# Second batch: masks written by TensorE and one exponential a pair; seven weight conversions in which ScalarE makes the three low bits

## The chip, the cores and the metric

The kernel runs on one core of one Trainium2 chip. The metric is the device time of one execution in microseconds (us), shown as the median of the runs. The kernel before takes 871.65 us, the median of three runs (871.54, 871.65 and 874.05).

## The reference

Eight batches, eight heads, 576 tokens, head size 64. Attention looks at 32 keys: the last 32 tokens in the first four heads, every fourth of the last 128 in the others. Its output, 4608 tokens of 512, goes through a feed-forward block with an ELU between two products. Everything is float32.

```python
scores = scale * q @ k.T                      # scale = 1/8, masked outside the window
attn = exp(scores - max(scores)); attn /= attn.sum(-1) + 1e-9
x = (attn @ v) as 4608 x 512
h = x @ w_in                                  # 512 x 2048
out = where(h > 0, h, exp(min(h, 0)) - 1) @ w_out    # 2048 x 512
```

The weights are drawn as float64, and are read from HBM as 64-bit integers. The kernel makes float32 of them itself.

## The kernel before, in words

Tokens go in chunks. The first chunks (`CS` = 3) have 512 tokens each; the later ones are done in another form that this change does not touch. A chunk's first product goes over 16 slices `f` of the inner 2048: `product1` makes h(f) in a PSUM bank (`h0` or `h1` in turn while c = 0), `elu` makes the ELU of it (ScalarE: Exp and then Relu; VectorE: the combination with h, at L632 or L634), and `second_product`, some slices later, adds that slice's four 128-token tiles to the four `o_ps` banks. The chunk c = 0, some 31 to 133 us into the span, has three more jobs beside these products:

- **Conversion of the weights.** `load_w` brings two slices of 64-bit words into a block `r` of a ring; a piece `j` (0 to 7) is four rows of such words. `magnitude` (L129, ScalarE, L136) reads the upper word of each as float32 and scales its exponent, into `a`. `convert` (L138) then runs three passes on VectorE: a shift left by 3 (L144), the sign from the upper word (L152), the three low bits from the lower word (L154). Piece 0 is done in parts of 512, 512 and 1024 columns, piece 1 in two parts of 1024, each later piece in one of 2048.
- **Splits.** From slice `F1` = 3 on, the weights and x are taken as a sum of two parts (cast on ScalarE L191, difference on VectorE L193; of x, `xall`, L589 and L590).
- **Attention of the second batch** (`second_attention`): four pairs of heads. Step E does the scores of a pair into the two `a_ps` banks and the beginning of its softmax (`exponentials`), X its end (`probabilities`), O the products with v. E0 stands behind slice 1, E1 behind 3, O0 behind 5, E2 behind 7, O1 behind 9, E3 behind 11, O2 and O3 behind 14 and 15. In `exponentials`, `masks_added` (L397, VectorE) adds the mask while it brings the scores from PSUM to the tile `sm`, of which there is one; L410 takes the maximum of 12 groups of 64 columns, L413 scales it, and L389 runs an exponential for each of the 12 groups on ScalarE, which also sums it. Then GpSimd normalises, VectorE transposes, and ScalarE and GpSimd copy to `pt`, which the products read.

The first batch's attention writes its masks by a matmul of an identity with the mask ahead of the scores (bf16, 96x384), which then add to it.

TensorE's order is the one in which the program is written (`mm` keeps it). The order on VectorE and ScalarE comes from a scheduler, apart from what is kept in place with `inorder` or held behind an instruction with `issue_after`. `masked` and `maxima` are two such instructions: the second part of a conversion is held behind the newest in `maxima`, the split of x for c = 0 behind `masked`.

Of the kernel before, what the change touches and what calls it, by code (L numbers as in the profile page):

```python
# [70 lines left out]
DOWN = 2.0 ** -112  # L71
# [3 lines left out]
def body(ctx: ExitStack, tc: tile.TileContext, q, k, v, masks, w_in, w_out, out):  # L75
    nc = tc.nc
# [12 lines left out]
    mask_sb = masks_sb[:, :2 * NU * 2 * G].rearrange("p (d m) -> p d m", d=2)  # L89
    ones_sb = masks_sb[:, 2 * NU * 2 * G:]  # L90
# [9 lines left out]
    raw2, raw, full4, full2, full = [None] * (NF // 2), [None] * NF, [None] * (NF // 2), [None] * NF, [None] * 2 * NF  # L100
# [9 lines left out]
    def mm(*args, **kw):  # L110
        return inorder(nc.tensor.matmul(*args, **kw))  # L111
# [12 lines left out]
    def words(j):  # L124

        u = raw2[j].rearrange("p t c -> p (t c)").bitcast(U32).rearrange("p (c two) -> p c two", two=2)
        return u[:, :, 0], u[:, :, 1]

    def magnitude(k):  # L129
        j, part = k // 2, slice(k % 2 * 2 * DM, (k % 2 + 1) * 2 * DM)  # L130
        if k % 2 == 0:
            full4[j] = wst.tile([P, 4, DM], F32, name=f"a{j}")
        full2[k] = full4[j][:, k % 2 * 2:k % 2 * 2 + 2, :]
        for t in range(2):
            full[need[2 * k + t]] = full2[k][:, t, :]
        return nc.scalar.activation(out=full4[j].rearrange("p t c -> p (t c)")[:, part], in_=words(j)[1][:, part].bitcast(F32), func=AF.Copy, scale=DOWN)  # L136

    def convert(j, keep=lambda ins: ins, part=slice(0, 4 * DM), behind=None):  # L138

        lo, hi = [u[:, part] for u in words(j)]  # L140
        a = full4[j].rearrange("p t c -> p (t c)")[:, part]
        au = a.bitcast(U32)

        keep(nc.vector.tensor_scalar(out=au, in0=au, scalar1=3, scalar2=None, op0=ALU.logical_shift_left))  # L144
        if behind is not None:

            with tc.issue_after(behind):
                return upper_and_lower(lo, hi, au, keep)
        return upper_and_lower(lo, hi, au, keep)

    def upper_and_lower(lo, hi, au, keep):
        keep(nc.vector.scalar_tensor_tensor(out=au, in0=hi, scalar=0x80000000, in1=au, op0=ALU.bitwise_and, op1=ALU.bitwise_or))  # L152

        return keep(nc.vector.scalar_tensor_tensor(out=au, in0=lo, scalar=29, in1=au, op0=ALU.logical_shift_right, op1=ALU.bitwise_or))  # L154
# [110 lines left out]
    qk_of, v_of = {}, {}  # L265
# [28 lines left out]
    def scores(s_ps, qt, kt, start):  # L294

        for n in range(NU):
            for c in range(GU):
                for h in range(2):
                    score(s_ps[h][:, n * 2 * G:(n + 1) * 2 * G], qt, kt, h, n, c, start, start or n == NU - 1)
# [38 lines left out]
    def first_attention(hp, loaded):  # L338
# [18 lines left out]
        if hp > 0:  # L357
            load_w(hp, mx)
        inorder(nc.vector.tensor_tensor(out=sm.rearrange("p (h n) j -> p h n j", h=2), in0=s4,
                                        in1=mx4.unsqueeze(3).broadcast_to([QB, 2, NU, 2 * G]), op=ALU.subtract))  # L360
        inorder(nc.scalar.activation(out=sm, in_=sm, func=AF.Exp, scale=0.125))
        yield
# [22 lines left out]
        a_ps = ps_f.tile([P, 2, TC], F32, name="db"[hp % 2])  # L385
        yield outputs(0, hp, [(a_ps[:, i, :], i * NA, (i + 1) * NA) for i in range(NU // NA)], vt, tr, inorder)

    def exponential(u, sm, nmx, sums):
        nc.scalar.activation(out=sm[:, u, :], in_=sm[:, u, :], func=AF.Exp, bias=nmx[:, u:u + 1], scale=0.125, accum_out=sums[:, u:u + 1])  # L389

    def masks_added(hp, places, sm, eng=nc.vector):

        dil = hp >= NPAIR // 2
        for i in range(max(len(p) for p in places)):
            for h in range(2):
                n0, n1, s_ps = places[h][i]
                last = eng.tensor_tensor(out=sm[:, h * NU + n0:h * NU + n1, :].rearrange("p n j -> p (n j)"), in0=s_ps[:QB, :(n1 - n0) * 2 * G],  # L397
                                        in1=mask_sb[:, int(dil), n0 * 2 * G:n1 * 2 * G], op=ALU.add)
        return last

    def exponentials(b, hp, places, sm=None):

        if sm is None:
            sm = ap.tile([QB, 2 * NU, 2 * G], F32, name="sm", bufs=1)
            last = masks_added(hp, places, sm)
            if b == 1:
                masked.append(last.ins)
        nmx = ap.tile([QB, 2 * NU], F32, name="nmx", bufs=4)
        sums = ap.tile([QB, 2 * NU], F32, name="sums", bufs=4)
        nc.vector.tensor_reduce(out=nmx, in_=sm, op=ALU.max, axis=mybir.AxisListType.X)  # L410
        if b == 1:

            maxima.append(nc.vector.tensor_scalar(out=nmx, in0=nmx, scalar1=-0.125, scalar2=None, op0=ALU.mult).ins)  # L413
            for u in range(NU):
                exponential(u, sm, nmx, sums)
        else:
            nc.vector.tensor_tensor(out=sm, in0=sm, in1=nmx.unsqueeze(2).broadcast_to([QB, 2 * NU, 2 * G]), op=ALU.subtract)
            nc.scalar.activation(out=sm, in_=sm, func=AF.Exp, scale=0.125)
            nc.vector.tensor_reduce(out=sums, in_=sm, op=ALU.add, axis=mybir.AxisListType.X)
        return b, hp, sm, nmx, sums  # L420

    def probabilities(b, hp, sm, nmx, sums):

        if b == 1:

            for u in range(NU, 2 * NU):
                exponential(u, sm, nmx, sums)
        normalise(nc.gpsimd if b == 1 else nc.vector, sm, sums, lambda ins: ins)
        tr = transposed()
        for r in range(2):  # L430
            part = sm[:, :, r * G:(r + 1) * G]
            nc.vector.transpose(out=part, in_=part)  # L432
            for c in range(GU):
                ks, cs, rs = slice((c + r) * G, (c + r + 1) * G), slice(c * G, (c + 1) * G), slice(r * G, (r + 1) * G)
                last_transpose[b] = (nc.gpsimd.tensor_copy if r else nc.scalar.copy)(out=tr[ks, :, cs], in_=sm[cs, :, rs]).ins  # L435
        return b, hp, tr
# [55 lines left out]
    def later_probabilities(b, hps, groups):  # L492
# [9 lines left out]
        def steps(j):  # L502
# [73 lines left out]
    masked, maxima = [], []  # L576
# [43 lines left out]
    def elu(h_ps, c, f, v=nc.vector, a=nc.scalar):  # L620
        e = fp.tile([P, TC], F32, name="e")
        if 0 < c < B - 1:
# [58 lines left out]
    o_of, done = {}, {}  # L681
# [222 lines left out]
    def second_attention():  # L904

        x32[1] = xp.tile([P, NPAIR, S], F32, name="x32", bufs=2)
        state = [None] * NPAIR

        for step in " E0 X0 E1 X1 O0  E2 X2 O1  E3 X3  O2 O3".split(" "):
            if step:  # L910
                what, hp = step[0], int(step[1])
                i = NPAIR + hp
                if what == "E":
                    s_ps = banks()
                    scores(s_ps, *qk_of.pop(i), True)
                    state[hp] = exponentials(1, hp, [[(0, NU, a)] for a in s_ps])
                    load_qk(i + 1)
                    if hp == 0:
                        load_v(i + 1)
                    if hp == NPAIR - 1:  # L920
                        load_qk(i + 2)
                elif what == "X":
                    state[hp] = probabilities(*state[hp])
                else:
                    b, _, tr = state[hp]
                    places = [(a, i * NA, (i + 1) * NA) for i, a in enumerate(banks())]
                    products(places, v_of.pop(NPAIR + hp), tr)
# [9 lines left out]
    for what in "m0 qk0 qk1 qk2 qk3 v0 v1 w0 v2 v3".split():  # L937
        i = int(what[-1])
# [12 lines left out]
    for what in "S0 S1 M0 M1 S2 P0 M2 T0 U0 S3 P1 P2 A0 M3 T1 U1 O0 T2 U2 P3 B0 O1 T3 U3 O2 G0 G1 O3 G2 A1 C0 D1".split():  # L951
        i = int(what[1])
# [17 lines left out]
    load_v(NPAIR)  # L970
    for j in range(2 * (NR - NE), 2 * NR + 2):
        load_w(j)
# [12 lines left out]
    for c in range(CS):  # L985
# [14 lines left out]
        for f in range(NF):  # L1000
            while c == 0 and ready < min(NF, f + AHEAD):
                for j in (ready, ready + 1):
# [56 lines left out]
            if f in when:  # L1059
                i = when.index(f)  # L1060
# [78 lines left out]
```

## Time and profile before

| | |
|---|---|
| median of 3 runs | 871.65 us |
| the profiled execution | 872.5 us |
| its span in the trace | 870.7 us |
| mean granted clock | 0.996 |
| TensorE busy | 853.7 us, 98% |
| VectorE busy | 555.7 us, 64% |
| ScalarE busy | 526.9 us, 61% |
| GpSimd busy | 75.0 us, 9% |

The profiled execution is 1.8 us longer than its span, and 0.85 us longer than the median. The rows of the trace give a start in us from the span's beginning, a length, and behind an arrow what ended an engine's idle time. Where work on an engine follows without a wait, one row's start lies a little ahead of the end of the row before it.

### The profile page before, as it was taken

Reading aid. Unit: us, or ns where it says so; the run is one execution under the profiler, and the core shown is the slowest. Engines: PE = TensorE matmul, PEld = TensorE weight load, DVE = VectorE, ACT = ScalarE, POOL = GpSimd, SP = SyncE. Lnnn points to the kernel's source line nnn. Section 1 sums busy time; section 2 is a strip of 40 time slices with the busy share of each in tenths; the row PEclk is TensorE's granted clock in tenths of the full one; section 3 lists DMA queues with packets and bytes.
Section 4 is the critical chain, followed back from the end, with each engine's and each line's share of the span. In section 5 each row is a group of like instructions: output and inputs, shape, how many; then the busy total and the mean of one; then the engine's idle time right before and its main releaser. Section 6 shows DMA issues by size and latency. Waiting matters only on the chain.

```text
span 870.7 us, 17559 instructions
## 1 busy us (share of the span) xinstructions
PE 853.7 (98%) x6788; PEld 722.5 (83%) x6788; DVE 555.7 (64%) x902; ACT 526.9 (61%) x1031; POOL 75.0 (9%) x112
## 2 busy tenths in 40 slices
PE   6999999999999999999999999999999999999998
PEld 4556878888878889888878898988899988999986
DVE  6899987766685857787765577545476635344431
ACT  3767987756585756667654575654566654555541
POOL 2013311000020200111010020100011100000000
PEclk8999999999999999999999999999999999999999
DMA  9997335134546346867753867662875652776441
GB/s 343 378 381 264 132 123 188 34 132 133 176 160 200 102 151 215 262 221 239 231 173 100 279 200 242 212 184 83 265 226 175 206 164 80 241 209 191 143 153 56
DMA packets 93459, 166.48 MB, mean 191 GB/s; under 512 B 9696, under 2 KB 40768, under 8 KB 93376
## 3 DMA queue, kind: packets, MB, share of 16 engines
q1 hardware_dynamic: 89200, 158.01, 57.0%
q10 hardware_dynamic: 4176, 7.34, 2.3%
q8 instruction: 54, 0.88, 0.4%
q14 instruction: 29, 0.24, 0.1%
HBM read 124.42 MB, written 40.89 MB: 190 GB/s over the span
## 4 chain that ended last, share of the span: by engine, by line
PE 84%; DVE 7%; ACT 4%; DMA 2%; issue 2%; POOL 1%; SPq 0%; ACTq 0%; DVEq 0%; POOLq 0%
PE o_ps L111 41%; PE h L111 34%; PE a_ps L111 8%; DVE a L152 1%; DMA out<-e 1%; POOL pt L435 1%; DVE a L154 1%; DMA r<-combined 1%; DVE nmx L410 1%; ACT sm L389 0%; ACT pt L383 0%; DVE sm L397 0%; PE a L111 0%; DMA kt<-k 0%; DVE a L144 0%
## 5 line engine op out<-in xcount | busy, mean ns | idle before, releaser
L111 PE MATMUL h<-xall,r 128*128 128x384 f32 (+1 forms) x708 | 156.9, 363 | 0.4 <-DVE e L634 0.2
L111 PEld LDWEIGHTS h<-xall,r 128*128 128x128 f32 x708 | 127.7, 188 | 17.2 <-issue 0.8
L111 PE MATMUL o_ps<-a,gh 128*128 128x512 f32 x394 | 129.0, 416 | 0.0
L448 DVE SCALAR_TENSOR_TENSOR a-1_3369<-a-1_3369,a 128x768 f32<-128x768 f32 x64 | 61.0, 953 | 87.9 <-ACT a L448 87.9
L111 PE MATMUL h<-r,r 128*128 128x384 f32 x476 | 108.3, 337 | 0.4 <-DMA r<-combined 0.4
L448 ACT COPY e<-h 128x384 f32<-128x384 f32 x96 | 46.0, 479 | 98.5 <-PE h L111 96.6
L111 PEld LDWEIGHTS o_ps<-a,gh 128*128 128x128 f32 x394 | 73.4, 188 | 21.8 <-issue 9.1
L448 ACT ACTIVATE a<-a-1_3369 128x384 f32<-128x384 f32 (+1 forms) x96 | 60.8, 634 | 50.0 <-DVE a-1_3369 L448 44.0
L111 PEld LDWEIGHTS h<-r,r 128*128 128x128 f32 x476 | 84.4, 188 | 4.0 <-ACT e L448 0.7
L111 PE MATMUL o_ps<-r,gh 128*128 128x512 f32 x242 | 75.4, 393 | 0.0
L111 PE MATMUL o_ps<-a,r 128*128 128x512 f32 x288 | 72.3, 392 | 0.0
L111 PE MATMUL o_ps<-a,gl 128*128 128x512 f32 x173 | 67.7, 391 | 0.0
L448 ACT ACTIVATE a<-a 128x768 f32<-128x768 f32 (+1 forms) x72 | 60.8, 845 | 1.9
L111 PEld LDWEIGHTS o_ps<-a,r 128*128 128x128 f32 x288 | 53.7, 188 | 9.9
L111 PE MATMUL h<-a,r 128*128 128x384 f32 x256 | 60.1, 336 | 0.0
L448 DVE TENSOR_TENSOR a-1_3369<-h,e 128x384 f32<-128x384 f32 x64 | 35.2, 550 | 34.8 <-PE h L111 34.7
L111 PEld LDWEIGHTS o_ps<-r,gh 128*128 128x128 f32 x242 | 44.9, 188 | 8.6
L111 PEld LDWEIGHTS h<-a,r 128*128 128x128 f32 x256 | 46.4, 188 | 4.2
L111 PE MATMUL o_ps<-r,gl 128*128 128x512 f32 x117 | 46.0, 393 | 0.2 <-DVE gl L448 0.2
L435 POOL COPY pt<-sm 32x384 f32<-32x384 f32 x36 | 32.9, 913 | 103.1 <-DVE sm L432 102.1
L111 PE MATMUL o_ps<-a,xall 128*128 128x512 f32 x153 | 39.5, 393 | 0.0
L637 DVE SCALAR_TENSOR_TENSOR e<-h,e 128x512 f32<-128x512 f32 x30 | 20.9, 696 | 27.1 <-ACT e L636 27.1
(219 smaller groups left out, 1553.6 us busy)
## 6 DMA issues: line engine op xcount, KB each, us to landing
r<-combined SPq DMA_DIRECT2D x224, 256.0 KB, 3.6
aside<-a-1_3369 SPq DMA_DIRECT2D x64, 192.0 KB, 3.4
vt<-v SPq DMA_DIRECT2D x30, 384.0 KB, 4.4
kt<-k SPq DMA_DIRECT2D x30, 304.0 KB, 4.9
qt<-q SPq DMA_DIRECT2D x30, 288.0 KB, 4.2
r<-w_in SPq DMA_DIRECT2D x16, 512.0 KB, 7.9
r<-w_out SPq DMA_DIRECT2D x16, 512.0 KB, 8.3
combined<-a SPq DMA_DIRECT2D x20, 256.0 KB, 3.2
```

The costliest lines, as they stand in the source:

```text
L111: return inorder(nc.tensor.matmul(*args, **kw))
L152: keep(nc.vector.scalar_tensor_tensor(out=au, in0=hi, scalar=0x80000000, in1=au, op0=ALU.bitwise_and, op1=ALU.bitwise_or))
L154: return keep(nc.vector.scalar_tensor_tensor(out=au, in0=lo, scalar=29, in1=au, op0=ALU.logical_shift_right, op1=ALU.bitwise_or))
L410: nc.vector.tensor_reduce(out=nmx, in_=sm, op=ALU.max, axis=mybir.AxisListType.X)
L435: last_transpose[b] = (nc.gpsimd.tensor_copy if r else nc.scalar.copy)(out=tr[ks, :, cs], in_=sm[cs, :, rs]).ins
L448: return lambda *args, **kw: inorder(getattr(self.eng, name)(*args, **kw))
L637: v.scalar_tensor_tensor(out=e, in0=h_ps, scalar=0.0, in1=e, op0=ALU.max, op1=ALU.subtract)
```

## The change

Masks: in step E of the second batch TensorE writes the mask into each bank first, and the scores add to it. VectorE takes the maximum of each bank straight from PSUM (6 groups), and subtracts it on the way to `sm`. ScalarE runs one exponential of 768 columns a pair, VectorE sums its groups. Conversions: for the pieces 1 to 7 `magnitude` issues one more pass on ScalarE, `low_bits`: it reads the upper 16 bits of each lower word as an integer, scales them so that rounding leaves the top three bits, and writes these over the low 16 bits of the upper word, in place. VectorE then needs one pass for the sign and the low bits together, in place of two.

```diff
+LOW = (1, 2, 3, 4, 5, 6, 7)
...
+    def low_bits(j, part):
+        h = raw2[j].rearrange("p t c -> p (t c)").bitcast(U16).rearrange("p (c four) -> p c four", four=4)[:, part]
+        return nc.scalar.activation(out=h[:, :, 2], in_=h[:, :, 1], func=AF.Copy, scale=2.0 ** -13, bias=2.0 ** -14 - 0.5)
...
-        return nc.scalar.activation(out=full4[j]..., in_=words(j)[1][:, part].bitcast(F32), func=AF.Copy, scale=DOWN)
+        done = nc.scalar.activation(out=full4[j]..., in_=words(j)[1][:, part].bitcast(F32), func=AF.Copy, scale=DOWN)
+        return low_bits(j, part) if j in LOW else done
...
+    def upper_and_lower(j, lo, hi, au, keep):
+        if j in LOW:
+            return keep(nc.vector.scalar_tensor_tensor(out=au, in0=hi, scalar=0x80000007, in1=au, op0=ALU.bitwise_and, op1=ALU.bitwise_or))
         keep(nc.vector.scalar_tensor_tensor(out=au, in0=hi, scalar=0x80000000, in1=au, op0=ALU.bitwise_and, op1=ALU.bitwise_or))
         return keep(nc.vector.scalar_tensor_tensor(out=au, in0=lo, scalar=29, in1=au, op0=ALU.logical_shift_right, op1=ALU.bitwise_or))
...
     def exponentials(b, hp, places, sm=None):
         if b == 1:
-            maxima.append(nc.vector.tensor_scalar(out=nmx, in0=nmx, scalar1=-0.125, scalar2=None, op0=ALU.mult).ins)
-            for u in range(NU):
-                exponential(u, sm, nmx, sums)
+            heads = [(slice(h * NU, (h + 1) * NU), a[:QB, :NU * 2 * G].rearrange("p (n j) -> p n j", n=NU)) for h, a in enumerate(places)]
+            for part, s3 in heads:
+                nc.vector.tensor_reduce(out=nmx[:, part], in_=s3, op=ALU.max, axis=mybir.AxisListType.X)
+                last = nc.vector.tensor_tensor(out=sm[:, part, :], in0=s3, in1=wide(nmx[:, part], NU), op=ALU.subtract)
+            masked.append(last.ins)
+            maxima.append(last.ins)
...
+        nc.scalar.activation(out=sm, in_=sm, func=AF.Exp, scale=0.125)
+        nc.vector.tensor_reduce(out=sums, in_=sm, op=ALU.add, axis=mybir.AxisListType.X)
...
     def probabilities(b, hp, sm, nmx, sums):
-        if b == 1:
-            for u in range(NU, 2 * NU):
-                exponential(u, sm, nmx, sums)
...
                     s_ps = banks()
-                    scores(s_ps, *qk_of.pop(i), True)
-                    state[hp] = exponentials(1, hp, [[(0, NU, a)] for a in s_ps])
+                    for a in s_ps:
+                        mm(a[:QB, :NU * 2 * G], ones_sb, mask_sb[:, int(hp >= NPAIR // 2), :], start=True, stop=False)
+                    scores(s_ps, *qk_of.pop(i), False)
+                    state[hp] = exponentials(1, hp, s_ps)
```

The scheduler places the new work. **ScalarE, from piece 1's two magnitudes to the third slice's Exp** (`r_281` and `a_538` are piece 1, `r_523` piece 2; `h_484`, `h_567`, `h_649` and, of the change, `h_648` are the slices 0, 1 and 2). Before:

```order
L136 ACTIVATE a_538<-r_281 128x1024 x2
L627 ACTIVATE e<-h_484 128x512
L629 ACTIVATE e<-e 128x512
L589 CAST xall<-x_142 128x512 x4
L627 ACTIVATE e<-h_567 128x512
L629 ACTIVATE e<-e 128x512
L136 ACTIVATE a_638<-r_523 128x1024 x2
L627 ACTIVATE e<-h_649 128x512
```

Now:

```order
L143 ACTIVATE a_538<-r_281 128x1024 x2
L633 ACTIVATE e<-h_484 128x512
L134 ACTIVATE r_281<-r_281 128x1024 x2
L635 ACTIVATE e<-e 128x512
L595 CAST xall<-x_142 128x512 x4
L633 ACTIVATE e<-h_567 128x512
L635 ACTIVATE e<-e 128x512
L143 ACTIVATE a_636<-r_523 128x1024 x2
L134 ACTIVATE r_523<-r_523 128x1024
L633 ACTIVATE e<-h_648 128x512
```

Two passes of `low_bits` (L134) stand between the Exp and the Relu of slice 0, and one ahead of the Exp of slice 2.

**VectorE, in the same place,** from the ELU of slice 0 (`gh<-h_484`) to the split of slice 3's weights (`h<-a_538`). Before:

```order
L632 SCALAR_TENSOR_TENSOR gh<-h_484,e 128x512
L144 TENSOR_SCALAR a_538<-a_538 128x1024
L590 TENSOR_TENSOR xall<-x_142,xall 128x512 x2
L152 SCALAR_TENSOR_TENSOR a_538<-r_281,a_538 128x1024
...
L152 SCALAR_TENSOR_TENSOR a_538<-r_281,a_538 128x1024
L193 TENSOR_TENSOR h<-a_538,h 128x512
```

Now (ahead of the first row stand the ELU of slice 0 and the first half's shift, as before):

```order
L596 TENSOR_TENSOR xall<-x_142,xall 128x512 x2
L421 TENSOR_REDUCE nmx<-a_ps_581 96x6
L421 TENSOR_REDUCE nmx<-a_ps_582 96x6
L161 SCALAR_TENSOR_TENSOR a_538<-r_281,a_538 128x1024
L152 TENSOR_SCALAR a_538<-a_538 128x1024
L596 TENSOR_TENSOR xall<-x_142,xall 128x512 x2
L422 TENSOR_TENSOR sm<-a_ps_581,nmx 96x384
L638 SCALAR_TENSOR_TENSOR gh<-h_567,e 128x512
L422 TENSOR_TENSOR sm<-a_ps_582,nmx 96x384
L161 SCALAR_TENSOR_TENSOR a_538<-r_281,a_538 128x1024
L152 TENSOR_SCALAR a_636<-a_636 128x2048
L204 TENSOR_TENSOR h<-a_538,h 128x512
```

Both halves of piece 1, the softmax work of the first pair and the shift of piece 2 now stand ahead of that split; one pass a half is gone.

**TensorE, ahead of the scores of each pair** (the first pair here). Before, the scores follow `h_567` at once. Now:

```order
L113 MATMUL h_567<-x_142,a_357 128x512 x4
L113 LDWEIGHTS masks_sb
L113 MATMUL a_ps_581<-masks_sb 96x384
L113 LDWEIGHTS masks_sb
L113 MATMUL a_ps_582<-masks_sb 96x384
L113 MATMUL a_ps_581<-kt,qt 32x64
```

Two matmuls with their weight loads are added a pair, eight in all; nothing else moves on TensorE, and nothing on GpSimd. On the DMA queue of SP a few loads of later batches and stores move past each other.

## Rows read from the trace of the kernel before

**Rows 1.** The page, part 1: busy time of each engine, its share of the span, and its instructions.

```profile
PE 853.7 (98%) x6788; PEld 722.5 (83%) x6788; DVE 555.7 (64%) x902; ACT 526.9 (61%) x1031; POOL 75.0 (9%) x112
```

**Rows 2.** The chain that ended last, in order of time (start in us, length in us, what): the first row of its stretch on VectorE, which goes from here to 116 us, and the row of TensorE that follows this stretch.

```profile
63.60 0.69 DVE gh L632
...
116.38 3.01 PE h L111 x12
```

**Rows 3.** Who waited for whom, on TensorE, from 28 us to the end: us in total, times, the longest.

```profile
PE h L111 <- ACT h L624: 1.4, 2, 1.2
PE h L111 <- DVE h L193: 1.0, 1, 1.0
PE h L111 <- DMA r<-combined: 0.4, 1, 0.4
PE a_ps L111 <- PE h L111: 0.3, 1, 0.3
...
PE h L111 <- DVE e L634: 0.2, 1, 0.2
```

**Rows 4.** The timeline of TensorE (start in us, length in us, engine, line, operation, output and input, shapes, count, and in brackets the idle time ahead of it).

```profile
36.44 0.97 PE L111 MATMUL a_ps<-kt,qt 64*32 64x64 f32 x72
37.34 3.70 PE L111 MATMUL h<-x,a 128*128 128x512 f32 x8
40.88 3.60 PE L111 MATMUL o_ps<-a,gh 128*128 128x512 f32 x8
44.48 2.11 PE L111 MATMUL h<-xall,h 128*128 128x512 f32 x8
47.63 1.19 PE L111 MATMUL h<-xall,h 128*128 128x512 f32 x4 [1.03 <-DVE h L193]
...
63.72 3.70 PE L111 MATMUL o_ps<-a,gh 128*128 128x512 f32 x8
...
70.00 3.59 PE L111 MATMUL o_ps<-a,gh 128*128 128x512 f32 x8
```

**Rows 5.** The timeline of ScalarE around slice 0: Exp, Relu, and the four casts of x.

```profile
34.93 0.58 ACT L627 ACTIVATE e<-h 128x512 f32<-128x512 f32 x1
35.54 0.63 ACT L629 ACTIVATE e<-e 128x512 f32<-128x512 f32 x1
36.08 2.17 ACT L589 CAST xall<-x 128x512 fp32r<-128x512 f32 x4
```

**Rows 6.** The timeline of VectorE in the same place, up to the split that TensorE waits for at 47.6 us, and the next piece's shift.

```profile
35.02 1.24 DVE L154 SCALAR_TENSOR_TENSOR a<-r,a 128x1024 uint32<-128x1024 uint32 x1
36.29 0.69 DVE L632 SCALAR_TENSOR_TENSOR gh<-h,e 128x512 f32<-128x512 f32 x1
36.89 0.68 DVE L144 TENSOR_SCALAR a<-a 128x1024 uint32<-128x1024 uint32 x1
37.49 1.29 DVE L590 TENSOR_TENSOR xall<-x,xall 128x512 fp32r<-128x512 f32 x2
...
46.89 0.68 DVE L193 TENSOR_TENSOR h<-a,h 128x512 fp32r<-128x512 f32 x1
...
48.71 1.21 DVE L144 TENSOR_SCALAR a<-a 128x2048 uint32<-128x2048 uint32 x1
```

**Rows 7.** Groups of instructions by line and form, 30 to 120 us: busy us and mean ns of one, then the idle time before them.

```profile
L136 ACT ACTIVATE a<-r 128x1024 f32<-128x1024 f32 x15 | 16.3, 1140 | 0.0
L389 ACT ACTIVATE sm<-sm,nmx 96x64 f32<-96x64 f32 x48 | 16.0, 338 | 9.3 <-DVE nmx L413 9.3
L154 DVE SCALAR_TENSOR_TENSOR a<-r,a 128x2048 uint32<-128x2048 uint32 x6 | 14.7, 2445 | 0.0
L397 DVE TENSOR_TENSOR sm<-a_ps,masks_sb 96x384 f32<-96x384 f32 x8 | 4.0, 545 | 2.1 <-POOL pt L435 2.1
L410 DVE TENSOR_REDUCE nmx<-sm 96x12 f32<-96x768 f32 x4 | 3.8, 940 | 0.0
L154 DVE SCALAR_TENSOR_TENSOR a<-r,a 128x1024 uint32<-128x1024 uint32 x3 | 3.7, 1219 | 0.1
```

**Rows 8.** Timelines of VectorE and ScalarE in the first batch's attention: a maximum taken from PSUM, and an exponential of 768 columns.

```profile
6.88 0.95 DVE L356 TENSOR_REDUCE nmx<-a 96x12 f32<-96x768 f32 x1 [6.88 <-PE a L111]
...
8.86 0.84 ACT L361 ACTIVATE sm<-sm 96x768 f32<-96x768 f32 x1 [6.84 <-DVE sm L359]
```

**Rows 9.** The timeline of TensorE in the first batch's attention: a wait, and the two matmuls that write the masks of a pair, and the scores that follow them.

```profile
13.75 1.21 PE L111 MATMUL c<-ident,sm 96*64 96x96 f32 x24 [2.27 <-DVE sm L328]
14.89 0.78 PE L111 MATMUL b<-masks_sb 96*96 96x384 bf16 x2
15.60 1.52 PE L111 MATMUL b<-r 64*32 64x64 f32 x72
```

**Rows 10.** Stretches of the span: length, busy us and count of each engine, TensorE's granted clock (behind POOL's column), share of the DMA engines, GB/s.

```profile
15.00:16.00 1.00, 1.00 (x26) 0.46 (x31) 1.00 (x2) 0.56 (x1) 0.00 (x0) 0.52 1.02 395
20.00:21.00 1.00, 1.00 (x16) 1.00 (x14) 0.72 (x2) 0.54 (x2) 0.37 (x2) 0.50 1.02 407
44.00:52.00 8.00, 6.96 (x92) 4.07 (x91) 7.97 (x9) 4.74 (x25) 0.00 (x0) 1.00 1.01 382
```

**Rows 11.** The timeline of TensorE later: matmuls of 384 columns at full clock, six and six.

```profile
409.35 1.20 PE L111 MATMUL h<-r,r 128*128 128x384 f32 x6
410.39 1.21 PE L111 MATMUL h<-xall,r 128*128 128x384 f32 x6
```

More of the change, by code (lines that the diff above doesn't have):

```diff
@@ L15 @@
 U32 = mybir.dt.uint32
+U16 = mybir.dt.uint16
 AF = mybir.ActivationFunctionType
@@ L135, in magnitude @@
             full[need[2 * k + t]] = full2[k][:, t, :]
-        return nc.scalar.activation(out=full4[j].rearrange("p t c -> p (t c)")[:, part], in_=words(j)[1][:, part].bitcast(F32), func=AF.Copy, scale=DOWN)
+        done = nc.scalar.activation(out=full4[j].rearrange("p t c -> p (t c)")[:, part], in_=words(j)[1][:, part].bitcast(F32), func=AF.Copy, scale=DOWN)
+        return low_bits(j, part) if j in LOW else done
     def convert(j, keep=lambda ins: ins, part=slice(0, 4 * DM), behind=None):
@@ L147, in convert @@
             with tc.issue_after(behind):
-                return upper_and_lower(lo, hi, au, keep)
-        return upper_and_lower(lo, hi, au, keep)
-    def upper_and_lower(lo, hi, au, keep):
+                return upper_and_lower(j, lo, hi, au, keep)
+        return upper_and_lower(j, lo, hi, au, keep)
+    def upper_and_lower(j, lo, hi, au, keep):
+        if j in LOW:
+            return keep(nc.vector.scalar_tensor_tensor(out=au, in0=hi, scalar=0x80000007, in1=au, op0=ALU.bitwise_and, op1=ALU.bitwise_or))
         keep(nc.vector.scalar_tensor_tensor(out=au, in0=hi, scalar=0x80000000, in1=au, op0=ALU.bitwise_and, op1=ALU.bitwise_or))
@@ L386, in first_attention @@
         yield outputs(0, hp, [(a_ps[:, i, :], i * NA, (i + 1) * NA) for i in range(NU // NA)], vt, tr, inorder)
-    def exponential(u, sm, nmx, sums):
-        nc.scalar.activation(out=sm[:, u, :], in_=sm[:, u, :], func=AF.Exp, bias=nmx[:, u:u + 1], scale=0.125, accum_out=sums[:, u:u + 1])
     def masks_added(hp, places, sm, eng=nc.vector):
@@ L404, in exponentials @@
             sm = ap.tile([QB, 2 * NU, 2 * G], F32, name="sm", bufs=1)
-            last = masks_added(hp, places, sm)
-            if b == 1:
-                masked.append(last.ins)
+            if b > 1:
+                masks_added(hp, places, sm)
         nmx = ap.tile([QB, 2 * NU], F32, name="nmx", bufs=4)
         sums = ap.tile([QB, 2 * NU], F32, name="sums", bufs=4)
-        nc.vector.tensor_reduce(out=nmx, in_=sm, op=ALU.max, axis=mybir.AxisListType.X)
+        wide = lambda x, n: x.unsqueeze(2).broadcast_to([QB, n, 2 * G])
         if b == 1:
-            maxima.append(nc.vector.tensor_scalar(out=nmx, in0=nmx, scalar1=-0.125, scalar2=None, op0=ALU.mult).ins)
-            for u in range(NU):
-                exponential(u, sm, nmx, sums)
-        else:
-            nc.vector.tensor_tensor(out=sm, in0=sm, in1=nmx.unsqueeze(2).broadcast_to([QB, 2 * NU, 2 * G]), op=ALU.subtract)
-            nc.scalar.activation(out=sm, in_=sm, func=AF.Exp, scale=0.125)
-            nc.vector.tensor_reduce(out=sums, in_=sm, op=ALU.add, axis=mybir.AxisListType.X)
+            heads = [(slice(h * NU, (h + 1) * NU), a[:QB, :NU * 2 * G].rearrange("p (n j) -> p n j", n=NU)) for h, a in enumerate(places)]
[4 more added lines that the diff above has]
+            maxima.append(last.ins)
+        else:
+            nc.vector.tensor_reduce(out=nmx, in_=sm, op=ALU.max, axis=mybir.AxisListType.X)
+            nc.vector.tensor_tensor(out=sm, in0=sm, in1=wide(nmx, 2 * NU), op=ALU.subtract)
+        nc.scalar.activation(out=sm, in_=sm, func=AF.Exp, scale=0.125)
+        nc.vector.tensor_reduce(out=sums, in_=sm, op=ALU.add, axis=mybir.AxisListType.X)
         return b, hp, sm, nmx, sums
     def probabilities(b, hp, sm, nmx, sums):
-        if b == 1:
-            for u in range(NU, 2 * NU):
-                exponential(u, sm, nmx, sums)
         normalise(nc.gpsimd if b == 1 else nc.vector, sm, sums, lambda ins: ins)
```

## The prediction

> **What bounds the kernel now.** I read the engines' busy time first: TensorE 98%, VectorE 64%, ScalarE 61% [rows 1]. Such a share is an average over stages, so the second view is the chain that ended last. It looks as if it spoke for the change: from 63.60 us it runs on VectorE almost alone up to 116 us [rows 2], where the conversions are. But a chain only tells what came last where somebody waited, and the third view, TensorE's waits, tells how much there is to win. From 28 us to the end they are 1.4, 1.0, 0.4, 0.3 and a few of 0.2 [rows 3], some 4 us in 843. In the chain's stretch TensorE repeats its pattern without a gap: eight matmuls for `o_ps`, then twelve for h, take 70.00 - 63.72 = 6.28 us [rows 4], and behind VectorE's long stretch it had waited 0.2 us. So VectorE is just in time there, not late. TensorE's own work sets the time from 36 us on. A gain can only come out of those waits; a loss comes from anything that adds work to TensorE or makes it wait anew.
>
> **What the change takes off VectorE and ScalarE.** VectorE loses the L154 pass of the pieces 1 to 7: six of 2445 ns and two of 1219 ns, 17.1 us, and eight mask additions of 545 ns, 4.4 us [rows 7]. It gains, a pair, two subtractions from PSUM (545 ns each by the additions' row) and one sum of groups (940 ns by L410's row); the two half maxima replace one of 940 ns at about the same cost (0.95 us for 768 columns from PSUM [rows 8], so some 0.5 each). That is 4 x 2.03 = 8.1 us back; VectorE ends some 13 us lighter. On ScalarE 48 exponentials go, 16.0 us [rows 7], and four of 0.84 us come [rows 8], 3.4 us. The fourteen `low_bits` passes (two a piece, 7 pieces) have no row. The nearest is `magnitude`, as many elements with the same stride on the input: 1.14 us [rows 7]. I take that, 16 us in all, so ScalarE comes out some 3 us heavier. As bounds: nothing excludes half of it, 0.57 us, for 16-bit elements, nor twice, 2.28 us, for the write that now has a stride too; I lean to the row because the number of elements is the same.
> The Trainium skill (ScalarE: Activation LUTs, section "What ACT_TABLE_LOAD costs") prices an ACTIVATE with immediate scale and bias at 186 ns + 0.833 ns a column, whatever the type. By it a pass would be an estimated 1.04 us, and the sum below would come out 0.2 us lower; no run here shows such a pass yet, and `magnitude`'s 1.14 us lies above it.
>
> None of this is on TensorE's path by itself: nearly all the relief falls where TensorE waited 0.5 us in all, between 50 and 130 us [rows 3].
>
> **Where the order puts the new passes.** ScalarE works in order, and two `low_bits` passes of piece 1 now stand between the Exp and the Relu of slice 0. Before, the Exp began at 34.93 and the Relu at 35.54 [rows 5]. Two passes of 1.14 us, less an overlap of some 0.07 us each, put 2.1 to 2.2 us in between: the Relu ends at about 38.3. The ELU `gh` of slice 0, which began at 36.29 [rows 6] when VectorE came to it, now waits for that until 38.35. Two things wait behind it. First, on VectorE everything that follows. Second, TensorE: `gh` is the read that frees the bank `h0` for the product of slice 2. That began at 37.34 [rows 4]. TensorE now comes there at 37.34 plus the two mask matmuls; `gh` ends at 39.04. **New wait: some 1.3 us, from 37.7 to 39.05**, and the first pair's mask matmuls lie inside it.
>
> **The next wait down the line.** TensorE goes on from 39.05 with 3.54 (slice 2), 3.60 (`o_ps`) and 2.11 us (eight of slice 3) [rows 4], and at 48.3 wants the second part of slice 3's split, for which it waited until 47.63 before. On VectorE, from `gh` at 38.35 in the new order, each start to start, that is the row's length less some 0.07 (36.29 + 0.69 against 36.89 [rows 6]): `gh` 0.6, shift 0.6, two of x 1.2, two maxima 1.0, the one remaining pass 1.15 [rows 7], shift 0.6, two of x 1.2, a subtraction 0.5, the next `gh` 0.6, a subtraction 0.5, the pass of the second half 1.15, and the shift of piece 2, 1.15 by the 1.21 of [rows 6]: 10.25 us. The split begins at 48.6 instead of 46.89, takes 0.68, and TensorE goes on at 49.3 instead of 47.63. **It is 1.65 us late there**, after a wait of about 1.0 us, as long as the old one: the pass saved on VectorE is eaten by the 2.1 us in which it stood still and by work that moved ahead of the split. ScalarE's cast for it comes in time (by 45.8, ahead of 46.2, when the first eight begin).
>
> **The masks.** Three more pairs lie where TensorE has no gap. Two such matmuls and their loads took 15.60 - 14.89 = 0.71 us [rows 9], but at half clock (0.52 to 0.50 [rows 10]). Six matmuls of as many columns take 1.04 us at full clock [rows 11], so two take 0.35. I take 0.4 with the loads: **3 x 0.4 = 1.2 us**; the bounds are 1.05 and 2.1.
>
> **What it gives back.** Behind 50 us VectorE gains on TensorE by a pass of 2.4 us for each piece. The 0.3 us before O0 (a bank that the mask addition held, because `sm` was still being copied) and the 0.2 us at 116 us should go: 0.5 us, less or more. The 1.4 us behind ScalarE's copy of h fall after c = 0, where neither engine's work changes; I leave them. SP's issues that move past each other are loads for later chunks; the one wait for a transfer is 0.4 us, for a tile that is not among them [rows 3].
>
> **The sum:** 1.65 + 1.2 - 0.5 = 2.35 us, 872.5 + 2.35 = 874.85 us for the profiled execution, whose span is 870.7. That execution lies 0.85 us above the median; against the median it is 871.65 + 2.35 = **874.0 us**. About 0.3%, or 2.6 us, is what a measurement here can tell from no change, so I forecast a small loss just short of it.
>
> **Rivals.**
> *The low-bits pass is dear, slower.* Place: the same Relu of slice 0. Every 0.1 us that a pass takes more delays `gh`, and with it TensorE, by 0.2 us. From 1.27 us a pass on, the loss is past 2.6 us; at 2.28 us it is 2.35 + 2.3 = 4.65, so 876.3 us, and a little more as the third pass delays the Exp of slice 2. For it: it writes two bytes of every eight, a form that no row shows. Against it: `magnitude` reads with that stride and still takes 1.14 us [rows 7]. Chance 0.17.
> *The clock falls, slower.* At 13.75 TensorE ended a wait of 2.27 us [rows 9], and in the rows from 15 to 21 us it had 1.2 GHz (0.5 of 2.4) [rows 10]. Six us at half clock are 3 us of its work. If the new wait does the same, the time is 874.0 + 3 = 877.0. Against it: the wait of 1.03 us at 46.6 was followed by 2.4 GHz throughout [rows 4, 10], and the new one is hardly longer. The Trainium skill (TensorE: Matmul & The Clock Gate, section "Why this matters for your kernels") asks for no idle gaps between bursts of matmuls, or the clock goes back to half; the two rows agree with such a rule, and do not tell on which side 1.3 us lies. Chance 0.07.
> *The relief wins, no loss.* If VectorE's stretch in the chain is worth more than the waits say, or the pass takes about 0.6 us, the wait for `h0` shrinks to nothing, and 1.0, 0.3, 0.2 and the 1.4 us later go too: 2.9 less 1.6 for all four pairs of masks is a gain of 1.3, so 870.3 us. For it: 13 us off an engine that was busy throughout. Against it: the order above, and that TensorE waited so little. Chance 0.15.
> *The change does not do what it says.* If the scheduler had left work where it was, only masks would count, +1.6; the order excludes that.
>
> **Chances.** Forecast 0.60, dear pass 0.17, clock 0.07, relief 0.15, something unseen 0.01. Of the forecast's own cases (a pass of 1.0 to 1.3 us, masks of 1.05 to 2.1 us) some four in ten lie past 2.6 us. Slower by over 0.3%: 0.24 + 0.17 = 0.41. Faster: even with every wait gone the gain stays under 2.6 us, so 0.03 for what I do not see. The rest, 0.56, is within 0.3%. The range, 871.0 to 877.0, holds the forecast with its bounds, most of the dear pass and the lower part of no loss.
>
> **What would show it.** A wait of TensorE for `gh` of 1 to 1.5 us near 38 us, a Relu two passes behind its Exp, passes of 1.0 to 1.3 us; the split that ends near 49.2 us with a second wait of about 1 us; mask pairs at 0.35 to 0.5 us; the same 1.4 us behind the copies of h; no wait between 50 and 130 us. I am wrong if TensorE passes 38 us without a wait, if the pass is far off 1.14 us, or if waits of over 1 us stand where I have none.

## The result and the profile after

The changed kernel takes 883.5 us (median of 4 runs, 881.56 to 884.88); the kernel before, on the same chip, 872.55 (4 runs, 871.54 to 874.05): a ratio of 1.0121, 95% interval 1.0097 to 1.0145. By the ratio that is some 10.5 us slower, above the range of 871 to 877.

The profiled execution took 882.7 us, its span is 880.9, 10.2 more than before. Busy time (page, part 1), to be read beside [rows 1]:

```profile
PE 856.7 (97%) x6796; PEld 724.0 (82%) x6796; DVE 543.8 (62%) x898; ACT 546.5 (62%) x953; POOL 70.9 (8%) x112
```

VectorE has lost 12 us, as planned; ScalarE has gained 20. Groups by line and form, 30 to 125 us, to be read beside [rows 7]:

```profile
L134 ACT ACTIVATE r<-r 128x1024 uint16<-128x1024 uint16 x14 | 34.1, 2533 | 0.0
L143 ACT ACTIVATE a<-r 128x1024 f32<-128x1024 f32 x15 | 16.4, 1144 | 0.0
L161 DVE SCALAR_TENSOR_TENSOR a<-r,a 128x2048 uint32<-128x2048 uint32 x6 | 13.7, 2288 | 9.8 <-ACT r L134 9.8
```

The first row is `low_bits`: 2.53 us a pass, where `magnitude` below it, with as many elements, takes 1.14. The third row shows who pays: VectorE, just in time before, now stands idle for 9.8 us waiting for that pass. TensorE's waits from 28 us to the end (total us, times, longest), to be read beside [rows 3]:

```profile
PE h L113 <- DVE e L640: 4.1, 2, 3.0
PE h L113 <- DVE gh L638: 3.6, 1, 3.6
PE h L113 <- ACT h L630: 1.2, 1, 1.2
PE h L113 <- DVE gl L454: 1.0, 1, 1.0
```

The waits for `gh` and `e` are those for an ELU. The first one, on ScalarE, VectorE and TensorE in turn (start, length, what), to be read beside [rows 4 to 6]:

```profile
34.84 0.59 ACT L633 ACTIVATE e<-h 128x512 f32<-128x512 f32 x1
35.31 4.77 ACT L134 ACTIVATE r<-r 128x1024 uint16<-128x1024 uint16 x2
39.81 0.70 ACT L635 ACTIVATE e<-e 128x512 f32<-128x512 f32 x1
```
```profile
40.54 0.69 DVE L638 SCALAR_TENSOR_TENSOR gh<-h,e 128x512 f32<-128x512 f32 x1 [4.37 <-ACT e L635]
```
```profile
36.26 0.49 PE L113 MATMUL a_ps<-masks_sb 96*96 96x384 bf16 x2
36.68 0.97 PE L113 MATMUL a_ps<-kt,qt 64*32 64x64 f32 x72
41.28 5.40 PE L113 MATMUL h<-x,a 128*128 128x512 f32 x8 [3.64 <-DVE gh L638]
46.52 3.60 PE L113 MATMUL o_ps<-a,gh 128*128 128x512 f32 x8
49.55 3.30 PE L113 MATMUL h<-xall,h 128*128 128x512 f32 x12
```

The two passes stand where the prediction put them, between Exp and Relu. They take 4.5 us there, not 2.2, so the wait is 3.64 us, not 1.3. And the eight matmuls behind it take 46.52 - 41.28 = 5.24 us instead of 3.54, because the clock fell to 1.2 GHz (in these stretches the granted clock is the number before the DMA share, 1.00 being 2.4 GHz; the two stretches left out have 0.50 and 0.70):

```profile
42.00:43.00 1.00, 1.00 (x2) 0.35 (x2) 1.00 (x3) 1.00 (x3) 0.00 (x0) 0.59 0.99 406
43.00:44.00 1.00, 1.00 (x2) 0.34 (x1) 1.00 (x4) 0.97 (x3) 0.00 (x0) 0.50 1.02 410
46.00:47.00 1.00, 1.00 (x4) 0.43 (x3) 1.00 (x3) 1.00 (x1) 0.00 (x0) 1.00 1.01 396
```

How far TensorE is behind can be read wherever both traces have the same work; here the product that follows c = 0's scores, then the first matmuls on `pt` and `vt` of two pairs. A window that ends there cuts off each row's length and count; the starts are what counts. Before, and after:

```profile
49.65 0.70 PE L111 MATMUL o_ps<-a,gh 128*128 128x512 f32 x1
89.00 0.39 PE L111 MATMUL a_ps<-pt,vt 128*64 128x96 f32 x4
119.33 0.47 PE L111 MATMUL a_ps<-pt,vt 128*64 128x96 f32 x6
```
```profile
54.01 2.41 PE L113 MATMUL o_ps<-a,gh 128*128 128x512 f32 x5
93.33 0.47 PE L113 MATMUL a_ps<-pt,vt 128*64 128x96 f32 x6
128.10 0.63 PE L113 MATMUL a_ps<-pt,vt 128*64 128x96 f32 x10
```

It is 4.36 us behind at 54 us, 4.33 at 93, 8.77 at 128, and 10.2 at the end. So there are two places: the first ELU, and a second loss of 4.4 us between 93 and 128. The second is these rows of ScalarE, VectorE and TensorE:

```profile
116.47 4.86 ACT L134 ACTIVATE r<-r 128x1024 uint16<-128x1024 uint16 x2
```
```profile
121.35 2.29 DVE L161 SCALAR_TENSOR_TENSOR a<-r,a 128x2048 uint32<-128x2048 uint32 x1 [1.90 <-ACT r L134]
124.43 0.68 DVE L640 SCALAR_TENSOR_TENSOR e<-h,e 128x512 f32<-128x512 f32 x1
```
```profile
110.95 3.03 PE L113 MATMUL h<-xall,r 128*128 128x512 f32 x12 [1.07 <-DVE e L640]
125.16 3.01 PE L113 MATMUL h<-xall,r 128*128 128x512 f32 x12 [2.99 <-DVE e L640]
```

Here the delay goes through VectorE: its pass of the conversion waits 1.90 us for the two passes of ScalarE, and the ELU that TensorE wants stands behind it. The wait of 1.07 us at 110.95 comes about in the same way, behind two passes that began at 103.14. The chain that ended last has no matmul from 31.1 to 125.2 us, and its largest share there is L134's, 28%. ScalarE is busy 72.4 of the 80 us from 50 to 130, against 64.9 before. The last 1.4 us come later; 1.0 of them is the wait for `gl` of L454.

### The profile page after: what moved, and what is told of

It reads as the page before. It is cut to its first block, busy times and chain, and to the rows that moved or that the text cites. A ratio compares the mean times of both kernels' runs of the same rounds, so it can differ in the third digit from the quotient of the medians.

```text
span 880.9 us, 17497 instructions
## 1 busy us (share of the span) xinstructions
PE 856.7 (97%) x6796; PEld 724.0 (82%) x6796; DVE 543.8 (62%) x898; ACT 546.5 (62%) x953; POOL 70.9 (8%) x112
## 4 chain that ended last, share of the span: by engine, by line
PE 82%; ACT 10%; DVE 3%; DMA 2%; issue 2%; POOL 0%; SPq 0%; ACTq 0%; DVEq 0%
PE o_ps L113 40%; PE h L113 34%; PE a_ps L113 8%; ACT r L134 3%; ACT a L143 1%; DMA r<-w_in 1%; DMA r<-combined 1%; DVE a L161 1%; ACT pt L441 1%; ACT e L633 1%; ACT r L202 0%; ACT e L635 0%; ACT pt L394 0%; ACT gh L648 0%; PE a L113 0%
## 5 line engine op out<-in xcount | busy, mean ns | idle before, releaser
L454 DVE SCALAR_TENSOR_TENSOR a-1_3343<-a-1_3343,a 128x768 f32<-128x768 f32 x64 | 61.0, 953 | 87.8 <-ACT a L454 87.8
L454 ACT COPY e<-h 128x384 f32<-128x384 f32 x96 | 46.0, 480 | 98.9 <-PE h L113 97.0
L454 ACT ACTIVATE a<-a-1_3343 128x384 f32<-128x384 f32 (+1 forms) x96 | 60.9, 634 | 51.1 <-DVE a-1_3343 L454 45.0
L454 ACT ACTIVATE a<-a 128x768 f32<-128x768 f32 (+1 forms) x72 | 60.8, 845 | 1.9
L454 DVE TENSOR_TENSOR a-1_3343<-h,e 128x384 f32<-128x384 f32 x64 | 35.2, 550 | 36.4 <-PE h L113 35.2
L113 PEld LDWEIGHTS o_ps<-a,gl 128*128 128x128 f32 x173 | 32.5, 188 | 6.8
```

Of the source, the lines that this page charges most:

```text
L454: return lambda *args, **kw: inorder(getattr(self.eng, name)(*args, **kw))
```

## The experiments

Theory P: all of it is the length of the low-bits pass, and the rest of the prediction's account holds. Rivals: the masks cost more than 1.2 us; the place of the passes, not their length, costs; some other part costs at 105 to 125 us.

**The masks and the one exponential alone** (no conversion changed):

```
-LOW = (1, 2, 3, 4, 5, 6, 7)
+LOW = ()
```

> The change without its conversions: masks on TensorE and one exponential a pair, VectorE's three passes a piece as before. Theory A (the loss is the low-bits pass, which took 2.53 us where 1.14 was taken): four pairs of mask matmuls at 0.42 us each, 1.7 us, less what ScalarE's saved 12 us give back in waits, so between -1 and +2 us of the kernel before. Theory B (the softmax's new form loses the time, by PSUM reads on VectorE and by its order): +5 us or more.

Measured: 877.06 us, ratio 1.0054 [1.0036, 1.0073], a loss of 4.7 us. TensorE's waits:

```profile
PE o_ps L113 <- DVE gl L649: 1.3, 1, 1.3
PE h L113 <- DVE h L204: 1.0, 1, 1.0
...
PE h L113 <- DVE gl L204: 0.6, 1, 0.6
```

That lies between the two theories, and above the 1.6 us that the prediction had for the masks with nothing else. This half by itself makes VectorE heavier. A pair gives up two additions of 0.545, a maximum of 0.94 [rows 7] and a scaling of 0.16 us, and gets two maxima of 0.53, two subtractions of 0.54 and a sum of 0.94: 0.9 us more, on an engine that is busy 57.2 of the 60 us from 50 to 110 here (56.3 before). So TensorE waits at two new places, 1.3 and 0.6 us, both for VectorE. With four mask pairs of 0.42 us that makes 3.6 us, of 3.3 by which the span of this execution (the fastest of the four) is longer.

**The conversions alone** (masks and exponentials of the kernel before; `LOW`, `low_bits` and `upper_and_lower` of the change):

> The change without its masks: seven pieces converted with a low-bits pass on ScalarE, the second batch's masks and its 48 exponentials as before. Theory A: ScalarE gets 14 x 2.53 = 35 us and loses nothing, so the loss is at least as large as that of the whole change, +10 to +15 us, with TensorE waiting 3.6 us for the ELU of slice 0 near 41 us and again between 105 and 130 us. Theory B: under +5 us.

Measured: 890.45 us, ratio 1.0211 [1.0194, 1.0228], a loss of 18.4 us, still more than theory A had. Waits of TensorE:

```profile
PE h L113 <- DVE e L645: 5.0, 2, 2.9
PE h L113 <- DVE gh L643: 4.0, 1, 4.0
PE o_ps L113 <- DVE gl L654: 2.9, 2, 2.1
PE a_ps L113 <- DVE sm L408: 1.9, 1, 1.9
```

Each half alone loses, and the losses do not add (4.7 + 18.4 against 10.5): the one exponential takes 12.6 us off ScalarE, where the passes go, and the conversions take 17 us off VectorE, where the masks' form adds work. In this run ScalarE is busy 57.6 of the 60 us from 50 to 110.

**A short pass** (the low bits are written for 412 of 1024 columns; in the others VectorE's pass takes the upper word's own three low bits, not zeros as the expectations have it; VectorE's work is the same):

```
-    ....rearrange("p (c four) -> p c four", four=4)[:, part]
+    ....rearrange("p (c four) -> p c four", four=4)[:, part][:, :412]
```

> The whole change, but each low-bits pass does only the first 412 of its 1024 columns (the other columns are left without their low bits), so that one takes about 1.14 us, as the prediction took it. Theory A: the pass's length alone is wrong, and the time comes near the forecast, +1 to +4 us of the kernel before, with a wait of 1 to 1.5 us for the ELU of slice 0. Theory C (the place of the passes between Exp and Relu, and the orders on VectorE that follow from it, whatever a pass takes): +6 us or more.

Measured: 873.78 us, ratio 1.0012 [1.0002, 1.0022]. The pass, and TensorE's first waits:

```profile
L134 ACT ACTIVATE r<-r 128x412 uint16<-128x412 uint16 x14 | 14.7, 1167 | 0.0
```
```profile
PE h L113 <- ACT h L630: 1.3, 1, 1.3
PE h L113 <- DVE gh L638: 1.0, 1, 1.0
```

At the length that the prediction took, its wait for `gh` is there (1.0 us, 1.3 predicted), the clock stays at 1.00, and neither 105 nor 125 us shows a wait. ScalarE's order around slice 0 is the same: Exp, two passes, Relu. In the program nothing but the pass is different, and 9.5 of 10.5 us are gone. But the scheduler does not keep every order: VectorE now does the first pair's two subtractions (1.0 us) behind the split of slice 3's weights, and the wait of TensorE for that split is 0.16 us. So this run alone doesn't part the length from the order; the two runs with the passes behind the Relu, below, do.

**Two more lengths**, 700 and 4 columns by the same edit (again the other columns get wrong low bits):

> The change with the low bits set for 700 of 1024 columns a pass (the rest keep their low bits zero). From 1.17 us at 412 columns and 2.53 at 1024 the pass should take about 1.81 us. Theory S (a straight price: each microsecond of pass costs the same, from 873.8 us at 1.17 to 883.5 at 2.53, 7.1 us a us): 878.4, within 2. Theory T (a threshold: nothing until TensorE's wait for the first ELU is long enough for the clock to fall behind it, then a jump): 874 to 876 when the clock stays at 1.00 in 38 to 47 us, 880 or more when it falls there. My prediction's own slope (0.2 us for each 0.1 us of pass): 875.1.

> The change with the low bits set for 4 of 1024 columns a pass (about 0.26 us a pass; the rest keep their low bits zero): what is left is the gain side of the change, VectorE's pass gone seven times and the one exponential a pair. If relief is worth anything when ScalarE pays next to nothing, the time is 868 to 871; if only the masks on TensorE (1.2 us) and nothing else shows, 873 to 874.5; by the straight price of 7.1 us a us it would be 867.

| columns | a pass, us | ratio | in 872 us | wait for `gh` |
|---|---|---|---|---|
| 4 | 0.21 | 0.9982 [0.9967, 0.9996] | -1.6 | none |
| 412 | 1.17 | 1.0012 [1.0002, 1.0022] | +1.0 | 1.0 |
| 700 | 1.81 | 1.0047 [1.0032, 1.0062] | +4.1 | 2.2 |
| 1024 | 2.53 | 1.0121 [1.0097, 1.0145] | +10.5 | 3.6 |

```profile
L134 ACT ACTIVATE r<-r 128x700 uint16<-128x700 uint16 x14 | 23.8, 1813 | 0.0
```
```profile
40.57 5.40 PE L113 MATMUL h<-x,a 128*128 128x512 f32 x8 [2.24 <-DVE gh L638]
```

At 700 columns the median is 877.9 us, at 4 it is 872.51 against 874.07. A microsecond of pass costs 2.7 us at first (2.6 / 0.96), then 4.8 (3.1 / 0.64), then 8.9 (6.4 / 0.72). By the intervals the last of these is dearer than the first; the middle one can't be told from either. The straight price (878.4) was right at 700 columns, but not at 4, where it had 867; a threshold with a jump had 880 or more with a fallen clock, and at 700 columns the clock does fall (5.40 us for the eight matmuls). My own slope, 875.1, was too low. With the length waits are added and grow: at 412 columns TensorE waits 1.0 us for `gh`; at 700, 2.2 for it and 1.2 for an ELU near 125 us; at 1024, 3.6 and 4.1. And with ScalarE paying next to nothing, all that this form of the change gains is 1.6 us, with the masks' time on TensorE in it; TensorE then waits for nothing between 28 and 130 us.

**The passes behind the newest Relu** (in `convert`, not in `magnitude`):

```
+        if j in LOW:
+            with tc.issue_after(below[-1]):
+                for o in range(part.start, part.stop, 2 * DM):
+                    low_bits(j, slice(o, o + 2 * DM))
```

> The whole change, with each piece's low-bits passes issued behind the newest Relu, so that slice 0's Relu comes ahead of the first two. Theory A: the 3.6 us wait near 41 us goes, but ScalarE still has 35 us of these passes, so waits for splits and ELUs remain later; loss +4 to +8 us. Theory C: the place was all, loss under +3 us.

Measured: 885.26 us, ratio 1.0146 [1.0131, 1.0161], a loss of 12.7 us, more than both theories had. The waits hardly differ from those of the change:

```profile
PE h L113 <- DVE e L644: 4.1, 2, 3.0
PE h L113 <- DVE gh L642: 3.3, 1, 3.3
```

The wait for an ELU has moved to the next one, that of slice 1. In this other place the long passes cost no less.

**The same with 412 columns:**

> Passes of 412 of the 1024 columns (the others are left without their low bits), and each piece's passes issued behind the newest Relu. If the rest of the short version's loss is its wait of 1.0 us for slice 0's ELU and the masks' 1.3 to 1.7 us, it loses that wait and comes within 1.5 us of the kernel before; if the passes' place did not matter there, it stays where the short version was, 1 to 2 us behind.

Measured: 873.43 us, ratio 0.9999 [0.9989, 1.0008]. The place is worth some 1 us (-0.1 here, 1.0 in the short version, with intervals that overlap), and there is still a wait for `gh` of 1.4 us, now that of slice 1. Taken together, in both places passes of 1.17 us cost about nothing to 1 us, and passes of 2.53 us cost 10.5 and 12.7: what decides is the length.

**Piece 1 as before** (`LOW = (2, ..., 7)`), so that no low-bits pass stands near slice 0's Relu:

> The whole change with piece 1 left on VectorE's three passes, so that twelve low-bits passes of 2.53 us are left, from piece 2 on. Theory A (two separate costs: the wait for slice 0's ELU and the clock behind it, some 5 us, and ScalarE's load, some 5 us between 105 and 130 us): the first goes and the second stays, +4 to +7 us of the kernel before. Theory L (one cost, ScalarE's load, that shows wherever TensorE first has to wait): as slow as the whole change, +9 us or more.

Measured: 885.0 us, ratio 1.014 [1.0123, 1.0157], a loss of 12.2 us, as theory L has it. Piece 2's passes come at 41.2 us instead, ahead of slice 2's Exp and of a cast, and TensorE waits there:

```profile
41.22 4.79 ACT L134 ACTIVATE r<-r 128x1024 uint16<-128x1024 uint16 x2
45.73 0.71 ACT L633 ACTIVATE e<-h 128x512 f32<-128x512 f32 x1
```
```profile
47.65 1.22 PE L113 MATMUL h<-xall,h 128*128 128x512 f32 x2 [3.02 <-ACT h L202]
```

The two losses, at 38 and at 125 us, thus have one source: two dear passes in a row hold up ScalarE for 4.5 us, and what TensorE needs next from it, or through VectorE, can be late. Not every pair costs: in the change those at 72.7 and 85.8 us were followed by no wait of TensorE up to 100 us.

**What is dear about the pass** (the kernel before, with eleven forms of ACTIVATE behind its end, three times over; their results are not used):

> The kernel before, with eleven forms of a ScalarE pass of 128x1024 appended at its end, three times each: the low-bits pass as it is, the same into another tile, without its bias, with a stride of 4 bytes in place of 8, with no stride, 16-bit input to contiguous float32, contiguous float32 to strided 16-bit and to contiguous 16-bit, the magnitude pass as it is, strided float32 to strided float32, contiguous 16-bit to contiguous float32. Their work is of no use to the result. Theory W (the write of two bytes in eight is what costs): forms that write strided 16-bit take about 2.5 us, those that write contiguous ones or float32 about 1.1 us, whatever they read. Theory R (the 16-bit integer read): all forms that read 16 bits take 2.5 us. Theory I (reading and writing the same tile): the form into another tile falls to 1.1 us. Theory D (16-bit integers in any layout): contiguous ones take 2.5 us too.

The rows of one round, in the order of the source (left out: the second and third, which write another tile and leave out the bias, 2.51 us each):

```profile
873.75 2.47 ACT L449 ACTIVATE r<-r 128x1024 uint16<-128x1024 uint16 x1 [4.55 <-DVE gh L679]
...
880.77 1.33 ACT L449 ACTIVATE r<-r 128x1024 uint16<-128x1024 uint16 x1
882.14 1.06 ACT L449 ACTIVATE r<-r 128x1024 uint16<-128x1024 uint16 x1
883.23 1.12 ACT L449 ACTIVATE r<-r 128x1024 f32<-128x1024 uint16 x1
884.38 2.47 ACT L449 ACTIVATE r<-r 128x1024 uint16<-128x1024 f32 x1
886.88 1.06 ACT L449 ACTIVATE r<-r 128x1024 uint16<-128x1024 f32 x1
...
889.12 1.10 ACT L449 ACTIVATE r<-r 128x1024 f32<-128x1024 f32 x1
```

They are: 16-bit read and write, each 8 bytes apart, in place; the same at a pitch of 4 bytes; of 2; a 16-bit read at 8 bytes to close 32-bit words (1.12: the read is free); close words to 16 bits at 8 bytes (2.47: the write is dear); close words to close 16 bits; then words 8 bytes apart read (1.12), and read and written (1.10). The eleventh, close 16-bit values read and close words written, takes 1.06. So of these forms only a 2-byte write that isn't close costs more, 2.5 us at 8 bytes and 1.33 at 4. A 4-byte write at the same 8 bytes does not. That is theory W, but for the 1.33 us.

**The three bits as a whole word**, to use that: the whole computation, with VectorE's two passes shared out anew.

```
-  activation(out=h[:, :, 2], in_=h[:, :, 1], ...)
+  activation(out=words(j)[0][:, part], in_=h[:, :, 1], ...)
-  tensor_scalar(out=au, in0=au, scalar1=3, op0=shift_left)
+  scalar_tensor_tensor(out=au, in0=au, scalar=3, in1=lo, op0=shift_left, op1=or)
-  scalar_tensor_tensor(out=au, in0=hi, scalar=0x80000007, ...)
+  scalar_tensor_tensor(out=au, in0=hi, scalar=0x80000000, ...)
```

> The change with another low-bits pass: ScalarE writes the three bits as a whole 4-byte word over the lower word, and VectorE's first pass is (shifted magnitude) OR that word, its second sets the sign; the whole computation is done. Theory W (what is dear is ScalarE's 2-byte write at a pitch of 8 bytes): the pass takes about 1.1 us for 1024 columns where it took 2.53, the wait of TensorE at 38 to 41 us and the half clock behind it go, and the time is 873.5 to 877; VectorE has about 1.0 us a conversion more to do than in the change, which can cost up to 3 us of that, as the masks alone did. Rival R (the 2-byte read at that pitch is as dear): the pass stays near 2.5 us and the time is 883 to 887. Rival V (the place of the pass on ScalarE costs, whatever its length): 880 to 885 with a pass of 1.1 us.

Measured: 879.75 us, ratio 1.0071 [1.0047, 1.0095]. The groups of the pass and of VectorE's first one, and the waits:

```profile
L134 ACT ACTIVATE r<-r 128x1024 uint32<-128x1024 uint16 x14 | 16.1, 1148 | 0.0
```
```profile
L153 DVE SCALAR_TENSOR_TENSOR a<-a,r 128x2048 uint32<-128x2048 uint32 x6 | 13.8, 2292 | 4.1 <-ACT r L134 4.1
```
```profile
PE h L113 <- DVE h L207: 2.7, 1, 2.7
PE h L113 <- ACT h L633: 2.4, 3, 1.2
PE h L113 <- DVE gh L641: 1.9, 2, 1.6
```

The length of the pass came out as expected, the time did not: it is 2.7 us above the end of my range, and only 0.25 below that of rival V. This run doesn't exclude V: the scheduler has put piece 1's passes between its magnitudes here, ahead of slice 0's Exp. Against V stand the short passes, which cost 1 us at most in both of their places. VectorE's first pass is now 2.29 instead of 1.35 us a piece (two sources); that of piece 2 (from 48.06 us, 2.28 long) stands right ahead of the split `h`, and TensorE waits 2.69 us for that split. It is the wait that the prediction had put there at 1.0 us. Beside the short pass (1.17 us on ScalarE, VectorE's shift as in the change) the difference is some 5 us (879.75 against 873.8, by the ratios). VectorE has 7 x 0.94 = 6.6 us more work, and its first pass now reads what ScalarE's pass writes, so it waits 4.1 us for it, where before only the second pass did. No run tells the shares of these two apart, nor that of the other order.

**The same with the masks of before:**

> The same word-wide low-bits pass and two VectorE passes, with the masks and exponentials of the kernel before. Theory W: with the 2-byte pass this half of the change gave 890.5; at 1.1 us a pass it gives 872 to 876, since ScalarE, which keeps the 48 exponentials of 16 us in all, gets 16 us instead of 35 and VectorE loses about 1.4 us a conversion. Rival R: 888 to 892, as with the 2-byte pass.

Measured: 881.99 us, ratio 1.0095 [1.0077, 1.0112]. By the ratios that is some 10 us less than with the 2-byte pass, for 14 x 1.39 = 19.5 us less on ScalarE (1.137 us a pass), but 6 above the end of what theory W had. VectorE has the same 0.94 us a piece more; here the split is waited for by 1.5 us and an ELU by 2.0. None of the versions that compute all that they must beats the kernel before.

## Why the prediction was wrong

**The failed step: the length of the low-bits pass.** It was taken as `magnitude`'s 1.14 us, with 2.28 as the upper bound "for the write that now has a stride too"; it is 2.53, outside both. I leaned to the row because the number of elements is the same. The forms show that this was the wrong likeness: `magnitude` writes close 32-bit words, and what is dear is the 2-byte write. Nothing in the trace of before had such a write, so the upper end should have been open and the rival heavier than 0.17. The Trainium skill (ScalarE: Activation LUTs, section "What ACT_TABLE_LOAD costs") gives one rate for fp32 and bf16 alike, an estimated 1.04 us here; the prediction's "whatever the type" goes beyond that. For 6 of the 11 forms the runs agree within 0.1 us, for a 2-byte write 8 bytes apart they measure 2.5, and the measurement decides.

**The second: what a microsecond of pass costs.** The rival "dear pass" counted 0.2 us for each 0.1, and gave 876.3 at 2.28 us. On the curve of the four lengths 2.28 us of pass cost about 8.3 us (4.1 + 6.4 x 0.47 / 0.72), so 880. I followed the delay at one ELU only. Fourteen such passes, on an engine that is then busy for 72.4 of 80 us, make later ELUs late too, at 111 and 125 us, where my list had "no wait between 50 and 130 us". Even with the bound in the sum, the range would have missed.

**The clock rival came true beside the dear pass.** I had taken them as alternatives, and the half clock as 3 us dear. It cost 1.7 (5.24 - 3.54). In the four lengths the two come together: behind waits of 2.24 and 3.64 us the rows show 1.2 GHz, behind 1.0 us 2.4 GHz. In the chances, too, the clock's 0.07 was left out of "slower", which by its own 877.0 us should have been 0.48 and not 0.41.

**What held.** The mechanism and its place: two passes between Exp and Relu, `gh` late, TensorE waiting for h0. At 1.17 us a pass the change costs 1.0 us [0.2, 1.9] where the sum had 2.35, and the wait is 1.0 where it had 1.3; that the sum is too high there goes with the wait for the split, 0.16 us and not 1.0, in an order of VectorE that isn't the one the prediction went through. The mask pairs take 36.68 - 36.26 = 0.42 us, as taken. The relief is worth little: a net 1.6 us with passes of 0.21 us, where the rival of no loss had 1.3 (870.3 us). The wait for the split at 49 us did not come in the change (probably because a wait of 3.64 us and half clock ahead of it gave VectorE time), but it came at 2.7 us in the version with whole words.

**What stays open.** Waits of 1.97 (whole words, old masks), 2.24 and 3.64 us that began near 38 us were followed by half clock, one of 1.64 us there (whole words) was not. But at 125 us a wait of 2.99 us had none behind it in the change, and one of 3.0 us at the same place had, with piece 1 as before (granted clock 0.61 from 127 to 130 us), as had one of 2.99 us there with the passes behind the Relu (0.57 from 126 to 130 us); nor had the 2.69 us for the split with whole words. The length of a wait alone does not tell them apart, and what does was not tried. It also stays open what the conversions would gain by themselves with a pass that costs next to nothing: the run with 4 columns has the masks in it.

## What to carry to other kernels

Price an added instruction by a row that has the same kind of write, not only as many elements; where no row has it, measure that one form by itself before moving work to it, and leave the upper end open. When work moves to an engine with slack on average, go through every later place where somebody waits for that engine, not only the first: here the price of a microsecond rose from 2.7 to 8.9 us. And check whether the engine that gives up work is one that anybody waits for: here each half of the change lost by itself, and even with passes of 0.21 us the whole won 1.6 us.

## What the runs showed of the hardware

- ScalarE, 1024 columns: a 2-byte write takes 1.06 us side by side, 1.33 us 4 bytes apart, 2.47 to 2.51 us 8 bytes apart (the last with a read of 16 bits 8 bytes apart as with one of close words); a 4-byte write 8 bytes apart takes 1.10 to 1.15 us.
- In place or to another tile, with a bias or without, the 2-byte write costs the same (2.47, 2.51, 2.51 us).
- VectorE's pass over 2048 columns of one source and close words took 1.35 us, with a second source 8 bytes apart 2.29 us. It is the second source that costs: over 1024 columns passes with two sources took 1.21 us with one of them 8 bytes apart (L161) and 1.22 us with both close (L204).
- Behind waits of TensorE of 1.97, 2.24, 3.64 and 3.97 us near 40 us (whole words with the old masks, 700 columns, the change, the conversions alone) eight matmuls of 512 columns took 5.24 us each time, 1.7 more than the 3.54 at 2.4 GHz.
